# GpSimd instead of VectorE adds the 1e-5 to the layer norm's variances, in an order mapped anew

## The chip, the cores and the metric

One core of a Trainium2 chip. The time is the device time of the whole launch in microseconds (us): the lower the better. A core has a matrix engine (TensorE, PE in the profile), three engines for elementwise work, VectorE (DVE), ScalarE (ACT) and GpSimd (POOL), a SyncE (SP) that here only issues DMAs, and 16 DMA engines. Every engine runs its own list of instructions in order; between engines there are semaphores.

## The reference

S = 2048 rows, D = 640 columns, F = 1536 hidden rows; everything that comes in or goes out is bf16.

```
x = A_q
g = sigmoid((x * gate_w).sum(-1))                 # one gate per row

k_shift[s] = sum over t of A_k[s-3+t] * shift_k[:, 3-t]     # 4 taps along the rows
kv = k_shift * A_v
y  = causal convolution of kv with ssm_k along S  # by rfft of length 4096, column by column
a  = x * (y + kv * ssm_D)

h = (x - mean(x)) / sqrt(var(x) + 1e-5)           # layer norm, along D
u = gelu(w1^T h + b1)                             # w1: 2048 x 1536, mixes the rows
b = w2^T u + b2                                   # w2: 1536 x 2048

out = g * a + (1 - g) * b
```

The 1e-5 of the change is the one in h.

## The kernel before

**How work is written and ordered.** The builder does not issue instructions where it describes them. Each operation goes into a plan with its engine, its operands and an estimate of its cost, through a few helpers: `ts` (tensor with one or two scalars; the profile gives its line, L660 with one scalar and L661 with two), `tt` (two tensors, L653), `act` (ScalarE, L691), `copy` (L668), `memset` (L671), DMAs (L265 on SP's queue, L262 for adding DMAs on GpSimd's queue, L722 and L728 for gathers and scatters of rows), and `pe` (a group of matmuls, L311). There are 853 operations. At the end `plan.run(ORDER)` (L1405; `run` is at L399) emits them in the order of a list written out by hand, `ORDER` (L433 to L470), which is a permutation of the 853 numbers. Since each engine runs its own instructions in the order in which they are emitted, `ORDER` sets the sequence on every engine and in both DMA queues, and also which of four PSUM slots a group of matmuls gets: `run` hands a group the free slot that was used longest ago. A tracker compares the operands of each operation with earlier ones and puts in the semaphore waits. The cost that an operation carries in the plan is not used when it is emitted.

**The layer norm (L901 to L933).** The 2048 rows are 16 tiles of 128 rows, in nine groups: two of one tile, then seven of two. For each group:

- SP loads x (L265).
- VectorE takes two statistics per tile, of 320 columns each (L919), and one aggregate per tile (L921), which leaves mean and variance in `mv`.
- `vpe` = variance + 1e-5, one `ts` for the group (L923, seen as L660), on VectorE.
- `rstd` = vpe to the power -0.5, on GpSimd (L924).
- h = (x - mean) * rstd: for 12 tiles by VectorE (L661), for 4 tiles (6, 10, 14 and 15) by ScalarE, for which VectorE first makes `nmr` = -mean * rstd (L661, 128x1).

**The other stages.** They run interleaved.

- *Filter.* `ssm_k` comes in four blocks of 512 (`wnat`). `w_turn` adds and subtracts mirrored halves on VectorE (`en`) and turns the result into `eo`, for the first two blocks by matmuls whose results ScalarE and VectorE evict in turn (L1006 is VectorE's eviction), for the others by a transposing DMA. `w_freq` multiplies `eo` with cosine and sine tables (`TFc`, `TFs`, with small ones like `TS`), and ScalarE evicts to `W`. The tables are made at the start from index tables (`idx`, `frow`, `hcol` on VectorE and GpSimd, sines on ScalarE); `AFc`, `AFs` are tables for kv alike.
- *kv.* `k` is loaded turned (`kT`), shifted and weighted by matmuls with diagonals (`dg`), evicted by ScalarE (`ks`), turned back by DMA (`kt`); VectorE multiplies it with `v` and forms `es`. `a_freq` (af0 to af3, one per block) multiplies with `AFc`/`AFs`, ScalarE evicts to `A`, VectorE adds A's sum.
- *Products.* `pair(j, m)` multiplies block j of kv's frequencies with block m - j of the filter's and accumulates in `Z` (VectorE, `tt` and `Z` by turns). `inverse(m)` multiplies Z with the inverse tables, and ScalarE evicts to `pq`.
- *MLP.* `mlp1` forms h^T w1 in four sets of three 128-row slices, accumulating over the 16 tiles of h, and ScalarE applies gelu (`gT`). `mlp2(q)` multiplies with `w2` in eight slices of 256 columns; two buffers take turns, so a slice's load (768 KB on SP's queue) can start only after the last matmul of the slice before the last. ScalarE evicts with scale 1 - g and bias.
- *Epilogue.* VectorE forms y from `pq`, multiplies with `xe` (x times the gate, by ScalarE), and the result is added to `out` by adding DMAs or, for odd groups of rows, by way of a scratch `rows_o`. For the last block VectorE adds everything itself (`fin`, L1327) and writes with two plain writes and two scatters.

**GpSimd's list around the layer norm** has, besides the nine powers, the index casts and masks of the start, the memset of 16 columns behind each `wnat` block, and small copies such as that of `TS`.

Of the kernel before, what the change touches and what calls it, by code (L numbers as in the profile page):

```python
# [12 lines left out]
ALU = mybir.AluOpType  # L13
# [409 lines left out]
def _checked(items, offs, base, top):  # L423
# [7 lines left out]


ORDER = [  # L433
# [36 lines left out]
]  # L470


def _build(nc, A_q, A_k, A_v, A_shift_k, A_ssm_k, A_ssm_D, B_x, B_w1, B_b1, B_w2, B_b2, gate_w, out):
# [18 lines left out]
    with ExitStack() as es:  # L492
# [152 lines left out]
        def nel(ap):  # L645
            k = 1
            for st, ct in list(ap.ap)[1:]:
                k *= ct
            return k
# [5 lines left out]
        def ts(out_, in0, s1, s2, op0, op1, pr, eng="DVE", cost=None):  # L655
            c = cost if cost is not None else (0.07 + nel(out_) / 1920.0 if eng == "DVE" else 0.4 + nel(out_) / 900.0)

            def f(e):
                if s2 is None:
                    return e.tensor_scalar(out_, in0, s1, None, op0=op0)  # L660
                return e.tensor_scalar(out_, in0, s1, s2, op0=op0, op1=op1)  # L661

            rr = [in0] + [a for a in (s1, s2) if isinstance(a, bass.AP)]
            return vop(eng, c, f, rr, [out_], pr, kind="ts")
# [105 lines left out]
        b = bufs  # L770
# [135 lines left out]
        for gi, (t0, cnt) in enumerate(groups):  # L906
            pr = 1.0 + t0 * 0.08
            plan.tag = f"ln{t0}"
            dma(x[:, t0:t0 + cnt, :], rows(A_q, t0, cnt, D, 0, D), f"x{gi}", pr)
            for t in range(t0, t0 + cnt):  # L910
                if LMODE[t] == "A":
                    act(h[:, t, :], x[:, t, :], ACT.Copy, pr, scale=-1.0 / (D * sq), acc=b["mv"][:, t, 0:1])
                    act(h[:, t, :], x[:, t, :], ACT.Square, pr, scale=1.0 / sq, bias=b["mv"][:, t, 0:1],
                        acc=b["mv"][:, t, 1:2])
                    continue
                for c in range(2):
                    o_ = b["stats"][:, t, c * 6:(c + 1) * 6]
                    i_ = x[:, t, c * HD:(c + 1) * HD]
                    vop("DVE", 0.393, (lambda o_, i_: lambda e: e.bn_stats(o_, i_))(o_, i_), [i_], [o_], pr, kind="bn")  # L919
                o_, i_ = b["mv"][:, t, :], b["stats"][:, t, :]  # L920
                vop("DVE", 0.11, (lambda o_, i_: lambda e: e.bn_aggr(o_, i_))(o_, i_), [i_], [o_], pr, kind="ba")  # L921
            sl = slice(t0, t0 + cnt)
            ts(b["vpe"][:, sl], b["mv"][:, sl, 1], 1e-5, None, ALU.add, None, pr, cost=0.07)  # L923
            vop("POOL", 0.7, (lambda o_, i_, e_: lambda e: e.tensor_tensor(o_, i_, e_, ALU.pow))(  # L924
                b["rstd"][:, sl], b["vpe"][:, sl], bc(c_mh, [[8, 128], [0, cnt]])), [b["vpe"][:, sl], c_mh], [b["rstd"][:, sl]], pr, kind="pow")
            for t in range(t0, t0 + cnt):
                if LMODE[t] == "D":
                    ts(h[:, t, :], x[:, t, :], b["mv"][:, t, 0:1], b["rstd"][:, t:t + 1],
                       ALU.subtract, ALU.mult, pr + 0.1, cost=0.36)
                else:  # L930
                    o_, a_, r_ = b["nmr"][:, t:t + 1], b["mv"][:, t, 0:1], b["rstd"][:, t:t + 1]
                    ts(o_, a_, r_, sq if LMODE[t] == "A" else -1.0, ALU.mult, ALU.mult, pr, cost=0.07)
                    act(h[:, t, :], x[:, t, :], ACT.Identity, pr, bias=o_, scale=r_)  # L933
# [504 lines left out]
```

## Time and profile before

| | us |
|---|---|
| three runs | 190.6, 190.5, 192.65 (median 190.6) |
| the profiled execution, whole time | 190.98 |
| its span (first to last instruction) | 189.2 |
| TensorE busy | 178.8 (95%) |
| VectorE busy | 175.5 (93%) |
| ScalarE busy | 125.5 (66%) |
| GpSimd busy | 35.2 (19%) |

How the rows that follow are read. `L660` is line 660 of the kernel. A row of a group reads: line, engine, operation, output <- inputs (partitions x elements, type), how often (x7), then after the bar the busy time of all in us, the mean of one in ns, and the idle time of the engine just before them with what ended it. A row of the timeline reads: start in us from the start of the span, duration in us, engine, line, operation, operands, count, and in brackets the idle time before it and its releaser. A row of the chain (start, duration, engine, operand) belongs to the chain of work that ended last, followed back from the last instruction. Rows with a stretch (`22.80:42.00`) give the length, the busy time of each engine with its instructions, the granted clock of TensorE, the share of the DMA engines and the GB/s. Rows of DMA issues give the queue, the KB each and the median time from issue to landing. Idle time of an engine that is not the bottleneck costs nothing.

### The profile page before, as it was taken

How to read it: one execution, taken by the hardware profiler on the slowest of the kernel's cores; microseconds unless marked ns; L12 is line 12 of the kernel's file. 1: busy time of each engine (PE TensorE's matmuls, PEld its weight loads, DVE VectorE, ACT ScalarE, POOL GpSimd, SP SyncE). 2: the span in 40 equal slices, each digit the busy share in tenths (PEclk: the TensorE clock that was granted, in tenths of full speed). 3: DMA queues.
4: the chain of work that ended last, by engine and by line, in shares of the span. 5: the costliest groups of instructions: out<-in, count | busy, mean ns of one | idle time of the engine just before them, and what ended most of it. 6: DMA issues, size and time to landing. Idle time of an engine off the chain costs nothing.

```text
span 189.2 us, 3940 instructions
## 1 busy us (share of the span) xinstructions
PE 178.8 (95%) x1590; PEld 123.0 (65%) x1590; DVE 175.5 (93%) x246; ACT 125.5 (66%) x202; POOL 35.2 (19%) x68
## 2 busy tenths in 40 slices
PE   7778899999999999999999999999999899999992
PEld 2345666566667757777767777777667577777771
DVE  7999999999999999999899999999999999997352
ACT  4978999787699489439823047706778482495930
POOL 8366076610000000101000000000005003110732
PEclk9999999999999999999999999999999999999999
DMA  5999999798996876787948998997988976979992
GB/s 155 315 325 272 130 152 282 221 222 190 236 326 129 196 202 181 151 248 164 232 67 221 231 243 197 219 242 205 309 280 224 225 226 221 232 215 240 175 166 69
DMA packets 81094, 40.37 MB, mean 213 GB/s; under 512 B 40051, under 2 KB 80884, under 8 KB 81076
## 3 DMA queue, kind: packets, MB, share of 16 engines
q1 hardware_dynamic: 78340, 37.18, 78.5%
q0 software_dynamic: 2736, 2.95, 9.3%
q8 instruction: 12, 0.20, 0.4%
q14 instruction: 6, 0.05, 0.1%
HBM read 26.03 MB, written 7.54 MB: 177 GB/s over the span
## 4 chain that ended last, share of the span: by engine, by line
PE 61%; DVE 22%; ACT 4%; issue 4%; DMA 4%; POOL 2%; POOLq 1%; DVEq 0%
PE pp L311 61%; DVE stats L919 6%; DMA w<-in_B_w_dram 4%; DVE v L653 3%; DVE en L653 3%; DVE es L653 2%; DVE idx L660 2%; DVE W L653 2%; ACT pq L691 1%; POOL rstd L924 1%; ACT xe L691 1%; DVE h L661 1%; DVE eo L1006 1%; DVE mv L921 1%; DVE A L653 1%
## 5 line engine op out<-in xcount | busy, mean ns | idle before, releaser
L311 PE MATMUL pp<-h,w 128*128 128x320 bf16 x384 | 57.1, 299 | 0.2
L311 PE MATMUL pp<-gT,w 128*128 128x320 bf16 x336 | 48.4, 299 | 0.9 <-DMA w<-in_B_w_dram 0.9
L311 PEld LDWEIGHTS pp<-h,w 128*128 128x128 bf16 x384 | 36.8, 98 | 15.9 <-issue 1.8
L311 PEld LDWEIGHTS pp<-gT,w 128*128 128x128 bf16 x336 | 32.6, 98 | 14.0 <-DMA w<-in_B_w_dram 1.4
L653 DVE TENSOR_TENSOR tt<-A,W 128x3840 bf16<-128x3840 bf16 (+2 forms) x16 | 27.8, 1738 | 0.3
L691 ACT ACTIVATE A<-pp 128x640 bf16<-128x640 f32 x32 | 21.3, 700 | 9.3 <-PE pp L311 9.3
L653 DVE TENSOR_TENSOR Z<-Z,tt 128x3840 bf16<-128x3840 bf16 (+1 forms) x14 | 26.2, 1868 | 0.2
L262 POOL DMA_DIRECT2D out_dram<-xe x3 | 3.8, 1252 | 73.0 <-DVE Z L653 68.4
L691 ACT ACTIVATE o<-pp,c,omg 128x640 bf16<-128x640 f32 x13 | 11.2, 881 | 6.8 <-PE pp L311 6.4
L691 ACT ACTIVATE ks<-pp 128x512 bf16<-128x512 f32 (+1 forms) x24 | 11.1, 518 | 6.1 <-PE pp L311 6.1
L691 ACT ACTIVATE gT<-pp,bf 128x640 bf16<-128x640 f32 x12 | 9.4, 792 | 8.2 <-PE pp L311 8.1
L691 ACT ACTIVATE xe<-xe,gg 128x640 bf16<-128x640 bf16 x16 | 12.7, 827 | 2.4 <-DMA xe<-rows_q 1.2
L919 DVE BATCH_NORM_STATS2 stats<-x 128x6 f32<-128x320 bf16 x32 | 13.7, 472 | 0.0
L653 DVE TENSOR_TENSOR Z<-A,W 128x3840 bf16<-128x3840 bf16 x6 | 12.8, 2154 | 0.9 <-PE pp L311 0.8
L691 ACT ACTIVATE pq<-pp 128x640 bf16<-128x640 f32 x16 | 10.3, 702 | 4.8 <-PE pp L311 4.8
L671 POOL MEMSET W<- 1x640 bf16 x4 | 2.7, 665 | 50.9 <-ACT nq L691 49.6
L691 ACT ACTIVATE W<-pp 128x640 bf16<-128x640 f32 x18 | 12.0, 722 | 0.1
L653 DVE TENSOR_TENSOR W<-W 128x2560 bf16<-128x2560 bf16 x8 | 11.9, 1486 | 0.0
L653 DVE TENSOR_TENSOR y<-pq 128x1280 bf16<-128x1280 bf16 (+1 forms) x10 | 6.6, 688 | 4.5 <-ACT pq L691 4.5
L311 PE MATMUL pp<-kT,dg 64*64 64x256 bf16 x320 | 10.5, 271 | 0.3 <-ACT Wo L691 0.3
L311 PE MATMUL pp<-eo,TFc 128*128 128x320 bf16 x48 | 8.9, 300 | 1.1 <-ACT TFc L691 1.1
L653 DVE TENSOR_TENSOR Z<-Z 128x1280 bf16<-128x1280 bf16 (+1 forms) x16 | 9.9, 653 | 0.1
(147 smaller groups left out, 303.6 us busy)
## 6 DMA issues: line engine op xcount, KB each, us to landing
w<-in_B_w_dram SPq DMA_DIRECT2D x24, 256.0 KB, 4.1
w<-in_B_w_dram SPq DMA_DIRECT2D x8, 768.0 KB, 5.1
wnat<-in_A_ssm_k_dram SPq DMA_DIRECT2D x4, 640.0 KB, 5.7
x<-in_A_q_dram SPq DMA_DIRECT2D x7, 320.0 KB, 6.3
out_dram<-o SPq DMA_DIRECT2D x6, 320.0 KB, 6.1
v<-in_A_v_dram SPq DMA_DIRECT2D x4, 320.0 KB, 4.5
rows_q<-in_A_q_dram SPq DMA_DIRECT2D x8, 160.0 KB, 3.2
xe<-in_A_q_dram SPq DMA_DIRECT2D x4, 320.0 KB, 5.8
```

The lines of the kernel that those rows point to most:

```text
L262: ins = engobj.dma_start(out_ap, in_ap, accum_op=ALU.add)
L311: ins = self.nc.tensor.matmul(ps_ap, lhsT=lhsT, rhs=rhs, start=start, stop=stop)
L653: return vop(eng, c, lambda e: e.tensor_tensor(out_, in0, in1, op), [in0, in1], [out_], pr, kind="tt")
L660: return e.tensor_scalar(out_, in0, s1, None, op0=op0)
L661: return e.tensor_scalar(out_, in0, s1, s2, op0=op0, op1=op1)
L671: return vop(eng, 0.03 + nel(ap) / 1200.0, lambda e: e.memset(ap, val), [], [ap], pr, kind="ms")
L691: return e.activation(out_, src, func, **kw)
L919: vop("DVE", 0.393, (lambda o_, i_: lambda e: e.bn_stats(o_, i_))(o_, i_), [i_], [o_], pr, kind="bn")
L921: vop("DVE", 0.11, (lambda o_, i_: lambda e: e.bn_aggr(o_, i_))(o_, i_), [i_], [o_], pr, kind="ba")
L924: vop("POOL", 0.7, (lambda o_, i_, e_: lambda e: e.tensor_tensor(o_, i_, e_, ALU.pow))(b["rstd"][:, sl], b["vpe"][:, sl], bc(c_mh, [[8, 12 ...
L1006: vop("DVE", 0.74, lambda e: e.tensor_copy(dst, src()), [src], [dst], 0.3, ps=[p_], kind="ev")
```

## The change

Two places. The addition of 1e-5 goes to GpSimd, where it stands ahead of the power that reads its result; the cost beside it is the plan's estimate. And `ORDER` is replaced by another permutation of the same 853 operations; of its 38 lines two are shown.

```diff
 ORDER = [
-    0, 3, 7, 10, 62, 1, 2, 5, 9, 8, 242, 13, 11, 241, 14, 31, 12, 206, 19, 137, 26, 4, 15, 21,
...
-    852, 844, 797, 792, 798, 793, 794, 848, 849, 838, 840, 839, 841,
+    0, 8, 5, 3, 7, 137, 2, 11, 1, 241, 4, 10, 6, 12, 153, 13, 14, 31, 32, 206, 21, 33, 285, 19,
...
+    832, 791, 843, 792, 836, 793, 844, 837, 794, 838, 840, 839, 841,
 ]
...
             sl = slice(t0, t0 + cnt)
-            ts(b["vpe"][:, sl], b["mv"][:, sl, 1], 1e-5, None, ALU.add, None, pr, cost=0.07)
+            ts(b["vpe"][:, sl], b["mv"][:, sl, 1], 1e-5, None, ALU.add, None, pr, eng="POOL", cost=0.25)
             vop("POOL", 0.7, (lambda o_, i_, e_: lambda e: e.tensor_tensor(o_, i_, e_, ALU.pow))(
                 b["rstd"][:, sl], b["vpe"][:, sl], bc(c_mh, [[8, 128], [0, cnt]])), [b["vpe"][:, sl], c_mh], [b["rstd"][:, sl]], pr, kind="pow")
```

The new list changes the sequence on every engine, far beyond the layer norm. What it does at the places that the prediction speaks of:

- *The start.* Ahead of VectorE's second eviction of `eo` the same 24 statistics stand in both orders, and 12 aggregates instead of 5; two additions fewer stand there, and the write to `AFs` stands ahead of it. Three statistics stand ahead of the third table's index.
- *The last groups of the layer norm.* GpSimd does two additions, three powers and the copy of `TS` in one run; VectorE has eight h and two `nmr` between its last aggregate and the h that reads the last power.
- *w2.* The numbers of matmuls between the last use of a w2 buffer and its next use are 48 to 66 (66 for the fifth slice, 56 before).
- *The third block.* One accumulation into Z and one y of the epilogue stand on VectorE between the last matmuls of af2 and the sum of its A.
- *The end.* 24 matmuls of `mlp2` stand behind the inverse of the last scatter's rows, instead of 12.

68 rows, old and new, of the table ORDER are left out of this document.

## The prediction, made before the changed kernel was run

> **What bounds the kernel now.** I read the page first, then the chain that ended last, then the busy time by stretches.
>
> ```profile
> span 189.2 us, 3940 instructions
> PE 178.8 (95%) x1590; PEld 123.0 (65%) x1590; DVE 175.5 (93%) x246; ACT 125.5 (66%) x202; POOL 35.2 (19%) x68
> ```
> ```profile
> 49.74 92.22 PE pp L311 x858
> 141.96 6.96 DMA w<-in_B_w_dram
> ...
> 148.96 23.55 PE pp L311 x172
> ```
> ```profile
> 8.20:22.80 14.60, 11.75 (x163) 8.14 (x163) 14.60 (x45) 12.67 (x22) 6.58 (x8) 1.00 1.14 260
> 22.80:42.00 19.20, 18.87 (x196) 12.14 (x192) 19.10 (x52) 17.42 (x32) 10.13 (x12) 1.00 0.95 211
> 42.00:58.00 16.00, 15.64 (x112) 10.40 (x110) 15.85 (x25) 13.19 (x21) 0.12 (x1) 1.00 0.90 244
> 58.00:148.00 90.00, 90.00 (x846) 64.32 (x843) 88.73 (x67) 54.19 (x94) 3.62 (x4) 1.00 0.87 210
> ...
> 149.00:185.50 36.50, 36.50 (x268) 26.04 (x268) 28.93 (x42) 21.68 (x29) 8.12 (x8) 1.00 0.86 201
> ```
>
> In the stretches the columns are TensorE, weight loads, VectorE, ScalarE, GpSimd, then the granted clock (1.00 throughout). Three things are to be seen. Up to 22.8 VectorE is busy in all 14.60 us and TensorE waits for it. From 22.8 to 185.5 TensorE is hardly ever idle: 0.33 us up to 42, 0.36 up to 58, nothing up to 148 or from 149 on; the chain shows what lies between, a load of w that the matmuls at 148.96 waited for. And VectorE stays close behind it (88.73 of 90 us). The matmuls of both kernels are the same, so the time is: when TensorE's dense run begins, its holes, and what lies behind its last matmul. The page's execution took 190.98 us, 1.78 more than its span, which I leave alone; it lies 0.4 above the median of the runs, 190.6.
>
> **The nine additions.** What leaves VectorE and what comes to GpSimd:
>
> ```profile
> L660 DVE TENSOR_SCALAR vpe<-mv 128x2 f32<-128x2 f32 x7 | 1.1, 155 | 0.0
> ```
> ```profile
> 23.19 0.26 DVE L921 BATCH_NORM_AGGREGATE mv<-stats 128x2 f32<-128x12 f32 x2
> 23.41 0.17 DVE L660 TENSOR_SCALAR vpe<-mv 128x2 f32<-128x2 f32 x1
> 23.49 0.20 DVE L921 BATCH_NORM_AGGREGATE mv<-stats 128x2 f32<-128x12 f32 x1
> ```
> ```profile
> L671 POOL MEMSET wnat<- 128x16 bf16 x4 | 0.5, 117 | 3.6 <-DVE mv L921 2.8 <-DVE en L653 0.8
> L668 POOL CAST hcol<-hcol_i 128x2 f32<-128x2 int32 x1 | 0.4, 357 | 0.0
> L660 POOL TENSOR_SCALAR idp<-id_i 128x128 bf16<-128x128 int32 x1 | 0.9, 854 | 0.0
> L924 POOL TENSOR_TENSOR rstd<-vpe,cst 128x2 f32<-128x2 f32 x7 | 5.3, 809 | 7.0 <-DVE vpe L660 6.9
> ```
>
> Seven additions take two tiles of rows, two more take one (the powers show the nine groups, below). On VectorE one is 0.155 us long, but the next instruction starts 0.08 us after it (23.41 to 23.49): instructions overlap there. Nine of them free 9 x 0.08 = 0.7 us, at most 9 x 0.155 = 1.4, at least nothing. The trace shows no such addition on GpSimd. Its nearest row is the cast of two columns, 0.357; the ends are the memset, 0.117, and the mask over 128 columns, 0.854. I take 0.36: same width, same count.
>
> Whether GpSimd then holds up h is decided at the last groups. In the changed order, counted from T, the end of VectorE's last aggregate, VectorE still runs eight of its h and two nmr before the h that needs the last power:
>
> ```profile
> 28.84 0.80 DVE L661 TENSOR_SCALAR h<-x,mv,rstd 128x640 bf16<-128x640 bf16 x2
> 29.55 0.20 DVE L661 TENSOR_SCALAR nmr<-mv,rstd 128x1 f32<-128x1 f32 x1
> ```
> ```profile
> L668 POOL COPY TS<-TFs 128x128 bf16<-128x128 bf16 x1 | 0.3, 287 | 0.1
> ```
>
> Two h take from 28.84 to 29.55, 0.355 each to the next start, and an nmr is 0.20 long, somewhat less to the next start: eight h and two nmr take 2.8 + 0.3 = 3.1 us. GpSimd begins its last run about 0.8 us before T (two h and an nmr lie between the last two aggregates) with two additions, three powers and the copy of TS: 2 x 0.36 + 3 x 0.81 + 0.29 = 3.4, done at T + 2.6. That is 0.5 us early, so I cost GpSimd's part at nothing. The cover is those eight h; with additions of 0.85 and powers of 1.08 (the longest, below) the run takes 5.2 and VectorE is 1.3 us late.
>
> Do the engines lengthen each other?
>
> ```profile
> 24.84 2.08 POOL L924 TENSOR_TENSOR rstd<-vpe,cst 128x2 f32<-128x2 f32 x3 [6.87 <-DVE vpe L660]
> 27.69 2.49 POOL L924 TENSOR_TENSOR rstd<-vpe,cst 128x2 f32<-128x2 f32 x3
> ```
> ```profile
> L661 DVE TENSOR_SCALAR h<-x,mv,rstd x12: 392/438/445, 26.5 to 32.7; 128x640 bf16<-128x640 bf16 x12
> L924 POOL TENSOR_TENSOR rstd<-vpe,cst x9: 561/698/1077, 10.8 to 29.2; 128x2 f32<-128x2 f32 x7, 128x1 f32<-128x1 f32 x2
> ```
>
> Three powers took 2.08 us beside VectorE's statistics and 2.49 beside its h; the longest single one was 1.077. The h beside them were not lengthened (392 to 445 ns). [...]
>
> **The new order: the start.** TensorE's dense run begins behind the second eviction of eo by VectorE:
>
> ```profile
> 21.60 0.81 DVE L1006 CAST eo<-pp 128x640 bf16<-128x640 f32 x1
> ```
> ```profile
> 5.54 0.49 DVE L660 TENSOR_SCALAR idx<-frow,hcol 128x512 int32<-128x512 int32 x1 [0.32 <-ACT adx L691]
> ```
>
> Ahead of this eviction the changed kernel has the same 24 statistics, but twelve aggregates instead of five, one write to AFs more and two additions fewer. An aggregate costs 0.11 (23.19 to 23.41 for two, with the next start): 7 x 0.11 + 0.07 - 2 x 0.08 = +0.7. Against it, three statistics now stand ahead of the third table's index, which covers the 0.32 us wait for ScalarE and some 0.2 of small waits behind it. Net +0.2. Seven of the nine additions stood behind this point: they are hidden by a TensorE that is busy 18.87 of the next 19.20 us. **+0.2**, bounds -0.5 and +0.7.
>
> **The wait for w2.**
>
> ```profile
> 148.96 1.26 PE L311 MATMUL pp<-gT,w 128*128 128x320 bf16 x8 [0.89 <-DMA w<-in_B_w_dram]
> 154.95 9.94 PE L311 MATMUL pp<-gT,w 128*128 128x320 bf16 x72
> ```
> ```profile
> 140.70 1.22 SPq L265 DMA_DIRECT2D rows_o<-xe  x2
> ```
> ```profile
> w<-in_B_w_dram SPq DMA_DIRECT2D x8, 768.0 KB, 5.1
> ```
>
> 72 matmuls take 9.78 us to the next start, 0.136 each. The fifth slice's load stood behind two writes of rows_o in SP's queue and took 6.96 us (chain); between the last use of its buffer and its first use stand 56 matmuls, 7.6 us. In the changed order these gaps are 48 to 66 matmuls: for this slice 66, 9.0 us, and for the shortest, the fourth, 48 and some small ones, 7.4 us, in which SP is held about 1 us by another load and a transfer, which leaves 6.4 for a median landing of 5.1. **-0.9**, bounds -0.9 and +0.5.
>
> **A new tight round trip.** The last matmuls of af2 feed VectorE's sum A, and all of its work up to the last Z feeds the last stage's inverse.
>
> ```profile
> 121.11 0.43 PE L311 MATMUL pp<-v,AFs 128*128 128x320 bf16 x2
> 122.32 1.49 DVE L653 TENSOR_TENSOR A<-A 128x2560 bf16<-128x2560 bf16 x1
> 123.73 2.15 DVE L653 TENSOR_TENSOR Z<-Z,tt 128x3840 bf16<-128x3840 bf16 x1
> ```
> ```profile
> 167.72 2.09 DVE L653 TENSOR_TENSOR Z<-Z 128x640 bf16<-128x640 bf16 x5
> ```
>
> Now VectorE needs 122.32 to 169.81, 47.5 us, and TensorE wants the last Z at 171.8, 50.2 us after 121.54. In the changed order one 2.15 us Z and one y of 0.74 stand ahead of A, so VectorE needs 44.6, with the eviction 45.4. TensorE has 324 matmuls of 128x320 between, 44.0, and 1.0 of gate work: 45.0. VectorE is late by 0.4. **+0.4**, bounds 0 and +2 (should a load of v hold VectorE on the way).
>
> **The end.**
>
> ```profile
> 185.27 1.01 DVE L1327 SCALAR_TENSOR_TENSOR xe<-pp,omg,xe 128x320 bf16<-128x320 f32 x2
> 185.64 1.01 POOL L728 DMA_INDIRECT out_dram<-xe,rev  x1 [3.53 <-DVE xe L653]
> 185.85 0.83 SPq L265 DMA_DIRECT2D out_dram<-xe  x2
> ```
> ```profile
> out_dram<-xe SPq DMA_DIRECT2D x2, 80.0 KB, 1.9
> out_dram<-xe,rev POOLq DMA_INDIRECT x2, 2.9
> ```
>
> The scatter lands at 185.64 + 2.9 = 188.5, the last plain write at about 188.3. In the changed order 24 matmuls (3.3 us) stand behind those of the last scatter instead of 12, so only the plain write is left: **-0.2**, bounds -0.3 and 0.
>
> **Sum.** +0.2 - 0.9 + 0.4 - 0.2 = -0.5: 190.98 becomes 190.5. The runs' median lay 0.4 lower than that execution; I forecast the middle, **190.3 us**: no change that 2% (3.8 us, about what a measurement of this kernel can tell from no change) would show.
>
> **Rivals.**
> *GpSimd becomes the bound of h (0.2), slower.* It decides from additions over 0.6 us: then the run passes the eight h. For it speaks 2.49 against 2.08, against it the 0.5 us of cover. VectorE is 1.3 late at the last h and 0.3 more where the memset of wnat stands behind two additions that wait for an aggregate (two of 0.85 and 0.1 against 1.5 us of VectorE work). All of it passed on: 190.3 + 1.6 = 191.9.
> *A transfer or buffer is late in the dense part (0.2).* TensorE has nothing to gain between 58 and 148, where its idle time is 0, and the new order sets every load anew. The wait for w2 stays (+0.9) and the round trip is late by its upper bound (+1.6): 192.8; two such places: 195.
> *Everything fits (0.12), faster.* Neither the round trip nor the 0.33 and 0.36 us of idle time return, and the start gains 0.5 instead of losing 0.2: 190.3 - 0.4 - 0.7 - 0.7 = 188.5.
>
> **How the numbers follow.** The forecast has 0.48, with 189.4 to 191.4 as its own range. From 188.6 to 193.6 the range takes in all of the first rival, most of the second and the edge of the third; some 0.15 is left out, most of it above. Slower by over 2% (above 194.4) is the second rival with two places: 0.1. Faster by over 2% (below 186.8) lies beyond the third: 0.04. Within: 0.86.
>
> **What would show it.** GpSimd's rows at the helper's line with vpe, near 0.36 us each; no vpe on VectorE; the second eviction of eo near 21.8 and TensorE's run on eo near 23.0; no wait of TensorE for w2; a wait of up to half a microsecond for Z at the inverse near 170; scatters that end ahead of the plain write. Wrong would make it: h waiting for rstd, VectorE idle between 26 and 32, or TensorE idle over 1 us anywhere from 58 on.

## The result and the profile after

The changed kernel took **191.72 us** (median of 22 executions, 190.78 to 194.49), the kernel before 190.41 (22 executions beside it, 190.11 to 192.65). The ratio is 1.0045, 95% interval 1.0024 to 1.0067: slower by 0.45%, where 0.2% faster was forecast. The time lies inside the stated range; the sign is wrong. (The ratio leaves out executions more than 1.5% above the fastest; the median of 22 has them in.)

Two things make up the 191.72. Eleven of the 22 executions ran with a mean granted clock of 0.985 or more; their median is 190.92, half a microsecond above before. The other eleven had 0.971 to 0.982 and took 191.36 to 194.49. Of the 117 executions of before that lie beside the experiments below, none had a clock under 0.991.

The profiled execution of the changed kernel took 190.81 us. Its page, first lines:

```profile
span 189.0 us, 3937 instructions
PE 180.1 (95%) x1590; PEld 124.2 (66%) x1590; DVE 175.4 (93%) x237; ACT 126.2 (67%) x202; POOL 36.8 (19%) x77
```

The busy time by stretches (TensorE, weight loads, VectorE, ScalarE, GpSimd, granted clock):

```profile
8.20:22.80 14.60, 11.66 (x141) 8.02 (x142) 14.60 (x50) 12.11 (x21) 8.42 (x17) 0.88 1.15 246
22.80:42.00 19.20, 18.16 (x199) 11.75 (x200) 19.02 (x38) 17.19 (x32) 9.49 (x17) 1.00 0.86 206
42.00:58.00 16.00, 16.00 (x117) 11.02 (x116) 14.81 (x20) 13.18 (x21) 0.00 (x0) 1.00 0.92 228
...
149.00:185.50 36.50, 36.50 (x270) 26.02 (x268) 29.49 (x41) 24.09 (x33) 8.24 (x8) 1.00 0.82 202
```

TensorE idles 1.04 us between 22.8 and 42 (0.33 before), and from 42 on there is no hole but 0.24 us. So the loss lies in the start, where the granted clock is 0.88 on the mean. The chain that ended last shows what the start hangs on:

```profile
9.04 1.46 POOL v L722
10.49 0.04 issue
10.53 1.61 POOL vpe L660
12.14 0.07 issue
12.21 0.72 POOL rstd L924
12.94 0.06 POOL TFs L671
12.99 0.46 POOL TFc L671
13.45 0.18 POOL TFs L671
13.63 0.05 issue
13.68 1.08 PE pp L311 x9
14.76 0.02 issue
14.78 0.70 ACT eo L691
15.48 0.81 ACT h L691
16.29 3.06 ACT Wo L691 x5
```

The first addition on GpSimd (`vpe`) took 1.61 us in this chain. Behind it on GpSimd stand a power and three memsets that finish the tables TFs and TFc; TensorE waited for the last of them until 13.68, and ScalarE had to evict later. Beside that addition VectorE ran this (timeline):

```profile
10.56 1.48 DVE L995 TENSOR_TENSOR dg<-id,shd 128x1280 bf16<-128x1280 bf16 x1
```

The other additions cost little: over the nine, the fastest, the median and the longest are 213, 227 and 1597 ns.

```profile
L660 POOL TENSOR_SCALAR vpe<-mv x9: 213/227/1597, 10.5 to 27.4; 128x2 f32<-128x2 f32 x7, 128x1 f32<-128x1 f32 x2
```

**The execution of before was not a typical one.** The forecast counted from 190.98 us, with 0.89 us of TensorE waiting for w2. A second profile of the same kernel, taken among the experiments, took 189.95 us (span 188.1). The last matmuls of before, of its second profile and of the changed kernel, in this order:

```profile
183.75 1.79 PE L311 MATMUL pp<-gT,w 128*128 128x320 bf16 x12
```
```profile
182.67 1.79 PE L311 MATMUL pp<-gT,w 128*128 128x320 bf16 x12
```
```profile
182.73 3.42 PE L311 MATMUL pp<-gT,w 128*128 128x320 bf16 x24
```

TensorE ends at 185.54, 184.46 and 186.15. Against the second profile the change costs 1.7 us up to the last matmul and gives 0.8 back behind it (188.1 - 184.46 = 3.6; 189.0 - 186.15 = 2.8): +0.9 in the span.

### The profile page after: what moved, and what is told of

It is laid out like the page before. It is cut to its first block, busy times and chain, and to the rows that moved or that the text cites. A ratio compares the mean times of both kernels' runs of the same rounds, so it can differ in the third digit from the quotient of the medians.

```text
span 189.0 us, 3937 instructions
## 1 busy us (share of the span) xinstructions
PE 180.1 (95%) x1590; PEld 124.2 (66%) x1590; DVE 175.4 (93%) x237; ACT 126.2 (67%) x202; POOL 36.8 (19%) x77
## 4 chain that ended last, share of the span: by engine, by line
PE 74%; DVE 12%; ACT 8%; POOL 3%; issue 2%; POOLq 0%; DVEq 0%
PE pp L311 74%; DVE Z L653 3%; DVE tt L653 2%; ACT Wo L691 2%; DVE v L653 2%; ACT h L691 1%; ACT eo L691 1%; POOL vpe L660 1%; DVE es L653 1%; DVE idx L660 1%; DVE A L653 1%; ACT ks L691 1%; POOL v L722 1%; DVE xe L653 1%; ACT TFs L691 1%
## 5 line engine op out<-in xcount | busy, mean ns | idle before, releaser
L262 POOL DMA_DIRECT2D out_dram<-rows_o x6 | 7.8, 1361 | 55.3 <-DMA rows_o<-xe 55.3
L311 PE MATMUL pp<-eo,TFs 128*128 128x320 bf16 x48 | 9.6, 329 | 2.8 <-ACT eo L691 2.0
L311 PEld LDWEIGHTS pp<-kT,dg 64*64 64x64 bf16 x320 | 8.1, 105 | 2.8 <-issue 1.6
```

The costliest lines, as they stand in the source:

```text
L262: ins = engobj.dma_start(out_ap, in_ap, accum_op=ALU.add)
L311: ins = self.nc.tensor.matmul(ps_ap, lhsT=lhsT, rhs=rhs, start=start, stop=stop)
```

## The experiments

Times in us; each ratio is to the executions of before on the same chip. "Low clock" counts executions with a mean granted clock below 0.985.

| kernel | n | median | fastest | low clock | ratio to before |
|---|---|---|---|---|---|
| the changed kernel | 22 | 191.72 | 190.78 | 11 | 1.0045 (1.0024 to 1.0067) |
| the same, again | 7 | 191.64 | 190.81 | 0 | 1.0057 (1.0030 to 1.0085) |
| new order, additions on VectorE | 12 | 190.52 | 190.18 | 2 | 0.9989 (0.9962 to 1.0017) |
| old order, additions on GpSimd | 12 | 192.11 | 191.69 | 0 | 1.0071 (1.0041 to 1.0102) |
| old start, new rest | 12 | 192.95 | 190.67 | 1 | 1.0067 (1.0030 to 1.0103) |
| new start, old rest | 12 | 192.29 | 191.13 | 4 | 1.0078 (1.0046 to 1.0109) |
| first addition alone on VectorE | 12 | 190.78 | 190.10 | 1 | 0.9992 (0.9966 to 1.0018) |
| table memsets ahead of it | 12 | 190.30 | 190.10 | 1 | 0.9978 (0.9947 to 1.0009) |
| the same, again | 12 | 190.37 | 189.87 | 3 | 1.0014 (0.9984 to 1.0043) |
| dg later | 12 | 190.68 | 190.30 | 1 | 0.9992 (0.9965 to 1.0020) |
| tables ahead and dg later | 12 | 190.69 | 190.35 | 3 | 1.0001 (0.9969 to 1.0032) |
| ten more matmuls | 12 | 191.51 | 190.73 | 0 | 1.0019 (0.9992 to 1.0045) |
| tables ahead, ten more matmuls | 12 | 190.37 | 189.94 | 0 | 0.9986 (0.9962 to 1.0010) |
| before with six matmuls fewer | 10 | 191.61 | 190.30 | 2 | 1.0031 (1.0001 to 1.0061) |

### Engine or order

The changed kernel's order with the additions on VectorE:

```diff
-            ts(b["vpe"][:, sl], b["mv"][:, sl, 1], 1e-5, None, ALU.add, None, pr, eng="POOL", cost=0.25)
+            ts(b["vpe"][:, sl], b["mv"][:, sl, 1], 1e-5, None, ALU.add, None, pr, cost=0.07)
```

> The changed kernel with its order kept and the nine additions back on VectorE. Two theories for the loss. THE ENGINE: the additions on GpSimd are what costs; in the trace of the changed kernel one of them took 1.60 us (10.53 to 12.13) beside VectorE's product dg, and the table memsets behind it on GpSimd made TensorE wait 0.43 us. Then this kernel loses that and runs at 190.4 us or below, against about 190.9 for the changed one at an undisturbed clock. THE ORDER: what costs is the new sequence of the first 31 us, whatever engine adds; then this kernel stays at 190.7 to 191.2, and the half granted clock between 10 and 14 us is there in some executions too.

190.52 us, ratio 0.9989: the loss is gone. None of the 12 executions is above 193 (7 of the 22 with the additions on GpSimd, but none of the 7 when that kernel was timed again, so their absence alone tells little). The new order alone is worth nothing either way that these runs can tell. The engine costs.

The old order with the additions on GpSimd (the same line, the other way round):

> The kernel before, its order kept, with the nine additions on GpSimd. THE ENGINE: slower than before by 0.5 to 1.5 us (190.8 to 191.8), with single additions of over 1 us beside VectorE's sums of two inputs. THE ORDER: the same as before within 0.3 us (190.0 to 190.6), since seven of the nine additions stand behind the point from which TensorE is dense.

1.0071: slower, by more than the upper end of the expectation in the median (192.11), and not by the way that was expected. No addition was longer than 0.45 us; VectorE waited for the powers instead (its waits, over the execution):

```profile
DVE nmr L661 <- POOL rstd L924: 0.9, 1, 0.9
...
DVE h L661 <- POOL TS L671: 0.7, 1, 0.7
DVE h L661 <- POOL rstd L924: 0.6, 1, 0.6
```

2.2 us of waits that the kernel before has none of (in the row with TS, too, the last power ends at 31.56, just before the h goes on). It is the first rival of the forecast, in the order of before: there GpSimd's additions and powers set the pace of h. That these waits make the loss is argued from this one profile. In neither profile of the changed kernel does an h wait for a power: its order has room for the longer chain.

Next, which part of the order. The orders were cut in two and crossed (the lists, written as formulas):

```diff
+ORDER = OLD[:242] + [i for i in NEW if i not in OLD[:242]]    # old start, new rest; additions on VectorE
```

> The first 242 operations in the order of before (up to the first matmuls on h, at 30.8 us there), all others in the new order, additions on VectorE. THE ORDER, with its loss in the start: the new start reaches the first matmuls on h 2.5 us later (33.9 against 30.8, less 0.6 for 16 matmuls that it has done by then), and the rest of the new order is the better one, so this kernel is the fastest of all, 188.4 to 189.5. If the new rest is no better than the old one: 190.1 to 190.9.

```diff
+ORDER = NEW[:229] + [i for i in OLD if i not in NEW[:229]]    # new start, old rest; additions on GpSimd
```

> The first 229 operations in the new order, all others in that of before, additions on GpSimd. THE ORDER, with its loss in the start: the slowest of all, 191.8 to 192.9, and a low clock in some executions. If start and rest weigh alike: 190.6 to 191.2.

The second came out as expected (192.29), the first did not: 192.95 instead of 188.4 to 190.9. Its profile, of its slowest execution (195.15 us), has waits of TensorE that are new or longer than in the profiles of its parents (the kernel before: 0.2 for es; the new order with the additions on VectorE: 0.6 for a load of w at the same place, the start of the MLP):

```profile
PE pp L311 <- DVE es L653: 1.7, 1, 1.7
PE pp L311 <- DMA kT<-in_A_k_dram: 1.4, 1, 1.4
PE pp L311 <- DMA w<-in_B_w_dram: 1.3, 1, 1.3
```

So crossing orders does not tell what a half is worth: the loads at the start of one half belong to the other. Nothing is concluded from these two.

### The one long addition

Only the first addition that GpSimd does goes back:

```diff
-            ts(b["vpe"][:, sl], ..., pr, eng="POOL", cost=0.25)
+            ts(b["vpe"][:, sl], ..., pr, eng="DVE" if t0 == 14 else "POOL", cost=0.25)
```

> The changed kernel; of the nine additions only the first that GpSimd does (group of tiles 14 and 15, at 10.53 us) goes back to VectorE, eight stay on GpSimd. THE ONE LONG ADDITION: the whole loss hangs on its 1.60 us, since the memsets of the tables stand behind it on GpSimd (the one that TensorE waits for ends at 13.6 us, and at 11.9 with all nine on VectorE); then this kernel is at 190.3 to 190.6 as with all nine on VectorE, and executions above 193 are gone. ALL NINE: the loss is the sum of many; then it stays above 190.75.

No execution is above 193 and the fastest is at 190.10, but the median, 190.78, is above what was expected; its ten slower executions spread from 190.63 to 191.55. That does not settle it. The next does: the memsets (operations 41, 39 and 43) go ahead of the addition (144), nothing else moves.

```diff
-    ..., 144, 56, 48, 259, 145, 208, 53, 267, 41, 39, 58, 105, 251, 43, 268, ...
+    ..., 41, 39, 43, 144, 56, 48, 259, 145, 208, 53, 267, 58, 105, 251, 268, ...
```

> The changed kernel, all additions on GpSimd; the three memsets of the tables TFs and TFc stand ahead of the first addition on GpSimd instead of behind its power. THE ONE LONG ADDITION, by way of what is queued behind it: 190.2 to 190.6, TensorE's wait for TFs (0.43 us) gone. If the addition costs by way of its power and h, or of VectorE being held: no gain, 190.75 to 191.

190.30 us, and 190.37 when it was run again; 0.9978 and 1.0014 against before, with all nine additions on GpSimd. GpSimd's timeline in it:

```profile
10.51 0.09 POOL L671 MEMSET TFs<- 1x1 bf16 x1
10.53 0.52 POOL L671 MEMSET TFc<- 1x512 bf16 x1
11.00 0.20 POOL L671 MEMSET TFs<- 1x128 bf16 x1
11.17 1.02 POOL L660 TENSOR_SCALAR vpe<-mv 128x2 f32<-128x2 f32 x1
12.28 0.72 POOL L924 TENSOR_TENSOR rstd<-vpe,cst 128x2 f32<-128x2 f32 x1
```

The addition is still long, and the memsets, beside the same product on VectorE, are not. TensorE's wait for TFs is gone from this profile, as expected. So the addition costs by what is queued behind it.

> The same kernel as new_tables_first, a second time, beside the changed kernel as it is. If its gain is real: 0.3 to 0.8 us below the changed kernel again, and at or below before (ratio 0.995 to 1.000). If it was chance: within 0.2 us of the changed kernel.

> The changed kernel as it is, timed beside the mended ones. Fastest executions at 190.8 as before, a third or more above 191.5 with a granted clock below 0.985.

The mended kernel stayed 1.27 us below the changed one on the same chip (190.37 against 191.64), which is above the expected 0.3 to 0.8; the expected low clocks of the changed kernel did not come (all seven at 0.991), its loss did.

Then the cause of the length: VectorE's product is moved behind other work of VectorE, 2.4 us of it by the trace (10.69 to 13.08; the expectations say 1.4).

```diff
-    ..., 145, 208, 53, 267, 41, ..., 148, 128, 250, 213, ...
+    ..., 145, 53, 267, 41, ..., 148, 128, 250, 208, 213, ...
```

> The changed kernel with VectorE's product dg (1.48 us, two inputs in memory) moved 1.4 us of VectorE's work later, so that the first addition runs beside statistics. If VectorE's product holds GpSimd up: this addition falls from 1.60 to 0.2 to 0.3 us, and the time to 190.3 to 190.6. If the addition is long for a reason of its own (the first of its kind on GpSimd): it stays above 1 us, and the time at 190.75 to 191.

```profile
10.54 0.26 POOL L660 TENSOR_SCALAR vpe<-mv 128x2 f32<-128x2 f32 x1
```
```profile
13.08 1.48 DVE L995 TENSOR_TENSOR dg<-id,shd 128x1280 bf16<-128x1280 bf16 x1
14.47 0.83 DVE L653 TENSOR_TENSOR en<-wnat 128x1280 bf16<-128x1280 bf16 x1
```
```profile
14.02 2.98 POOL L924 TENSOR_TENSOR rstd<-vpe,cst 128x1 f32<-128x1 f32 x2
```

1.60 became 0.26: the addition is long because of the product beside it. And the stall has moved: the two powers that now fall beside the product and the sums behind it took 2.98 us (1.51 in the changed kernel). The time, 190.68, is a little above what was expected. Both mends together:

> Both mends: the table memsets ahead of the first addition, and VectorE's product dg moved 1.4 us of work later. If the addition matters by what is queued behind it on GpSimd alone, moving dg as well brings nothing: 190.0 to 190.4, like the tables alone. If the length of the addition itself matters too (its power, ScalarE's h of tile 14): 189.6 to 190.0.

190.69 is above both expectations. It is 0.3 above the tables alone in the median, but its ratio to before, 1.0001, is not above theirs, 1.0014: no difference that these runs can tell. Taking the length off the addition brings nothing once the memsets are ahead of it.

The end of the addition goes with that of the product: in the changed kernel the addition ended at 12.13 and the product at 12.04; with the memsets first, 12.19 and 12.11. Each time it ended 0.08 to 0.09 us behind the product, whenever it had started; in the changed kernel it had even started 0.03 us ahead of the product (10.53 and 10.56). The memsets, which have no input, ran beside the product at their usual length: 0.52 and 0.20 with the memsets first, 0.52 and 0.23 in the changed kernel, where the product had ended. By what the product holds the addition up is not shown.

### The clock

```diff
-    NWARM = 15
+    NWARM = 20
...
         pe([p_], [(p_, 0, 512, wz, wzb, True, True)] * NWARM, -400, cost=0.427 * NWARM + 0.9)
+        p_ = _PS()
+        pe([p_], [(p_, 0, 512, wz, wzb, True, True)] * 5, -400)    # ahead of the first matmuls on eo
```

> The changed kernel with ten more matmuls on the constant wz whose results nobody reads: five at the end of the fifteen at the start, five between the second group of turning matmuls (8.5 us) and the first ones on eo (10.4 us), where TensorE idles. THE CLOCK: the half granted clock between 10 and 14 us comes from TensorE's idle time between 7.4 and 10.4 us; then it is gone in nearly all executions (clock 0.995 or more), and with it the executions above 191.3; the fastest stay at 190.8, since there the clock is full already. If the clock falls for another reason, it falls here as often, in about half of the executions below 0.985.

No execution is below 0.985 and none above 191.85, and the fastest is at 190.73, as expected; five of the twelve still have 0.989 to 0.991, where nearly all were expected at 0.995 or more. The median is 191.51, and the clock is not what keeps it high (seven executions at 1.00 took 190.73 to 191.61). Its profile names another cause: VectorE waited for the third block of the filter.

```profile
40.53 1.58 DVE L653 TENSOR_TENSOR en<-wnat 128x1280 bf16<-128x1280 bf16 x2 [1.36 <-DMA wnat<-in_A_ssm_k_dram]
```

That block's buffer lies where `mv` and `nmr` lay, so its load goes out when the last h is done. In the changed kernel (ScalarE's last h, then SP's issue):

```profile
33.35 0.93 ACT L691 ACTIVATE h<-x,nmr,rstd 128x640 bf16<-128x640 bf16 x1
```
```profile
34.38 0.37 SPq L265 DMA_DIRECT2D wnat<-in_A_ssm_k_dram  x1
```
```profile
38.90 1.58 DVE L653 TENSOR_TENSOR en<-wnat 128x1280 bf16<-128x1280 bf16 x2
```

4.5 us from issue to use. In the kernel before the issue stands at 33.21 and the use at 39.65, 6.4 us; in the new order with the additions on VectorE the issue stands at 33.41. A late start thus leaves this load less room. In the kernel with the ten matmuls it was issued at 34.50 and could be used at 40.53, 6.0 us later, and VectorE waited. This is shown in one profile. The changed kernel's second profile comes from its executions at 191.4 to 192.3 (191.64) and has no such wait, so the load doesn't explain them all; there the time was lost at the start, as the clock shows below.

What the clock follows was tried from both sides. First before, with TensorE idle earlier:

```diff
-    NWARM = 15
+    NWARM = 9
```

> The kernel before, its order and its additions kept, with nine matmuls on the constant wz at the start instead of fifteen (their results are not read), so that TensorE idles from about 4.9 to 8.2 us instead of from 6.9. THE CLOCK FOLLOWS TENSORE'S IDLE TIME: the granted clock of most executions falls from 0.996 to 1.000 to below 0.992, by a stretch of about 3.3 us at half clock, and the time rises by 0.3 to 2 us. If the clock falls for another reason than idle time: clock and time as before (190.2 to 190.8).

Five of ten executions had 0.973 to 0.991, and the median rose by 1.1 us. Its profiled execution (190.8 us of span, clock 0.973):

```profile
5.00:8.00 3.00, 0.00 (x0) 0.00 (x0) 2.68 (x8) 2.94 (x5) 1.66 (x8) 0.88 1.04 316
8.00:11.00 3.00, 2.77 (x23) 2.39 (x24) 3.00 (x16) 2.49 (x5) 0.29 (x2) 0.50 1.09 360
11.00:14.00 3.00, 2.10 (x9) 0.95 (x8) 3.00 (x8) 2.09 (x4) 2.80 (x4) 0.50 1.15 312
14.00:17.00 3.00, 3.00 (x13) 1.68 (x12) 3.00 (x11) 1.57 (x3) 2.55 (x3) 0.50 1.13 251
17.00:20.00 3.00, 3.00 (x23) 1.92 (x22) 1.30 (x3) 2.16 (x5) 0.95 (x1) 0.91 1.14 233
```

That is half of them, where most were expected. TensorE was busy for 0.00 us from 5 to 8, and at 8 the clock was down. The clock fell as forecast, but the lost time is not the clock's: the other five executions show 1.00 and took 191.4 to 192.2 us (median 192.00), more than the five with the lower clock (191.10). One candidate was not tried, the start itself. The fifteen matmuls on wz took 4.99 us in one profile (the second with the memsets ahead) and 6.37 in another (the second of before), while the granted clock shows no fall there in either: the second of before has 1.000 over the whole execution, and what the other lacks (0.991) lies between 11 and 15 us (0.57, 0.50, 0.50 and 0.72). So in these two profiles the granted clock doesn't tell how fast the start ran. Then the mended new order with the ten matmuls more:

> The changed kernel with the table memsets ahead of the first addition and with ten more matmuls on wz at the start (five behind the fifteen, five before the first ones on eo; their results are not read). THE CLOCK FOLLOWS TENSORE'S IDLE TIME: no execution below 0.985 (3 of 12 and 1 of 12 without the ten), and the time of the best ones of the tables alone, 190.1 to 190.4, in nearly all. If not: a clock of 0.97 to 0.985 in some executions as before.

All twelve executions are at 0.999 or 1.000, as expected; their times, 189.94 to 191.12, spread further than the 190.1 to 190.4 that were expected of nearly all. As far as these runs show it, the clock goes with how busy TensorE is at the start: from 8 to 11 us it was busy for 2.38 us in the profile of this kernel (clock 1.00) and for 1.30 and 1.31 in the two of the changed kernel (0.991 both). By what the five executions at 1.00 of the kernel with fewer matmuls lost their time stays open. In the changed kernel's first profile the stretch at half clock is one of 3.42 us: the clock was 0.72, 0.50, 0.50 and 0.57 of full in the four microseconds from 10 to 14 (0.56 + 1 + 1 + 0.86, if it was full or half). In the second profile of the changed kernel the fall came later, behind a longer wait for the memset:

```profile
13.67 0.72 PE L311 MATMUL pp<-eo,TFs 128*128 128x320 bf16 x4 [1.72 <-POOL TFs L671]
```
```profile
14.00:15.00 1.00, 0.67 (x8) 0.41 (x6) 1.00 (x3) 0.30 (x1) 0.84 (x3) 0.93 1.28 232
15.00:18.00 3.00, 2.54 (x10) 1.49 (x11) 3.00 (x12) 2.59 (x5) 1.83 (x3) 0.50 1.12 264
18.00:19.00 1.00, 1.00 (x8) 0.64 (x6) 1.00 (x4) 0.67 (x2) 0.00 (x0) 0.86 1.04 338
```

0.14 + 3 + 0.28 = 3.42 us again, now over matmuls that were due: the matmuls that wait for W at 28.36 in the first profile do so at 29.25 in the second, 0.9 us later. Both profiles have 0.991, one stretch each; the profile with 0.973 has 10.26 us at half (0.72 + 9 + 0.54 by the rows from 5 to 20), three times as long. A stretch is not a loss by itself: with the additions on VectorE five of the twelve executions have 0.990 or 0.991, and they took 190.18 to 190.48 us.

In the changed kernel TensorE had not been idle all the time ahead of the falls. These are the 3.41 us, about the length of a fall, before the one at 10.44 (11 - 0.56) and before the one at 14.86 (15 - 0.14); the first number behind the comma is TensorE's busy time:

```profile
7.03:10.44 3.41, 1.12 (x13) 0.60 (x12) 3.41 (x13) 2.22 (x5) 1.52 (x2) 1.00 0.97 303
```
```profile
11.45:14.86 3.41, 1.50 (x16) 0.96 (x14) 3.41 (x12) 2.06 (x4) 3.16 (x9) 1.00 1.27 268
```

TensorE was busy for 1.12 and 1.50 us of the 3.41. What sets off a fall, and why the changed kernel has 0.973 in one execution and 1.000 in another, no run here shows.

### Before once more

> The kernel before, for a second profile. The forecast took off 0.9 us for TensorE's wait for the fifth slice of w2, as the one profiled execution showed it (190.98 us, above the median 190.4). If that wait belongs to every execution: 0.7 to 1.0 us again. If it belongs to that execution: below 0.5 us, and with it a time near 190.3.

No wait for w2 at all, 189.95 us. The profiles of the old order with the additions on GpSimd and with six matmuls fewer have none either (their waits for w, where there is one, stand at the start of the MLP). The 0.89 belonged to that one execution.

None of these kernels beats the kernel before beyond its interval; the best, with the table memsets ahead, are level with it.

## Why the prediction was wrong, step by step

- **"I cost GpSimd's part at nothing" is the step that failed.** It was argued at one place, the last groups of the layer norm, and there it held: no h waited for a power in either profile, and GpSimd's last power ended 2.84 us after VectorE's last aggregate (29.77 against 26.93), where 2.6 was forecast. What the step left out is the other end of GpSimd's list: three table memsets that TensorE needs stand behind the first addition, which took 1.60 us, and TensorE waited for them until 13.68.
- **The price of an addition, 0.36 with ends 0.117 and 0.854,** held for eight (the median of the nine is 0.227) and missed the ninth, whose 1.60 is nearly twice the upper end. The two rows that read memory, the cast and the mask, come from moments without a long two-input operation on VectorE (it made the index table, 2.34 to 4.06 us, from one tensor at a time, and the first statistics). Whether the engines lengthen each other was looked at for powers beside statistics and h (2.08 and 2.49 us for three), and h was found unharmed (392 to 445 ns); the operation to look for was dg, of 1.48 us.
- **The rival with GpSimd as the bound** (0.2, 191.9) had the right engine, but the wrong place: in the changed kernel it decides at the start by way of the tables, not at h, so that 191.9 lies close to the median is luck. At h it decides in the old order.
- **The start, +0.2.** The second eviction of eo came at 21.97, as forecast (21.8). But TensorE was no longer bound by it: its dense run on eo began at 24.40 instead of 23.0, behind ScalarE, which was late from the tables on.
- **The wait for w2, -0.9.** Right that no such wait is in the changed kernel's profiles, wrong that it was there to be won: the second profile of before has none. The term was measured on an execution 0.4 us above the median, and the text saw that difference without asking which of its waits made it.
- **The round trip to the last inverse, +0.4:** no wait near 170. VectorE's work behind af2 was the bound at an earlier place: the chain that ended last runs from the matmuls ahead of 124.45 by way of A and VectorE's list to the matmuls on v at 145.10, where TensorE waited 0.24 us.
- **The end, -0.2:** the direction was right and the size too small. 3.6 us behind the last matmul became 2.8, with the last scatter issued 1.5 us ahead of TensorE's end (184.64) instead of 0.1 behind it (185.64 in the first profile of before), so that the plain write is the last to land (two issued from 186.18 on, 1.6 us to landing in the median; the scatter, at 2.9, by about 187.5).
- **The clock** was taken as 1.00 throughout and no row was thought to change it. The changed kernel's executions below 0.985 took 0.4 to 3.6 us more than the median of its others; how much of that is the clock's is not shown.
- **What a measurement can tell** was put at 2%, 3.8 us. The 22 executions of each kernel told 0.45% from no change.

Summed as measured against the second profile: +1.7 up to the last matmul, -0.8 at the end. With the additions on VectorE the same order is level with before within its interval, and so it is with them on GpSimd and the table memsets ahead; so what is lost is the first addition's.

## What to carry to other kernels

When an operation moves to another engine, look at everything that is queued behind each of its instances on that engine, first of all at the start, and at what the neighbour engine runs at that moment: one addition of nine, by the memsets behind it, cost what was lost here. Before a wait in a profile is counted as a gain, ask whether a typical execution has it; a profile slower than the median by half of the wait was the sign here that it doesn't. Look at the clock behind a gap of TensorE too: in the second profile of the changed kernel one of 1.72 us was followed by 3.42 us at half clock over matmuls that were due, and the matmuls that wait for W came 0.9 us later than in the first, where the fall was over at 13.86.

## What was not expected of the hardware

- An addition over 128 x 2 numbers on GpSimd took 1.60 us beside a product of two inputs on VectorE (the changed kernel) and 0.26 when the product came later; the median of the nine is 0.227. Two powers took 2.98 us beside that product and the sums behind it, instead of 1.51. Memsets beside the same product kept their length (0.52 and 0.20, against 0.52 and 0.23).
- The granted clock fell to one half for 3.42 us in both profiles of the changed kernel, and for 10.26 us in that of before with six matmuls fewer; in the changed kernel TensorE was busy for 1.12 and 1.50 us of the 3.41 before, the second 44%. In the changed kernel 17 of the first 22 executions and all seven later ones have a clock of 0.991 or less; of the 117 of before four have 0.991 and none less. Between 7 and 10 us TensorE was busy for 1.14 and 0.73 us in the two profiles of the changed kernel, for 1.64 and 2.08 in those of before.
- Six matmuls on a constant, left out at the very start, cost the kernel before 1.1 us in the median (ratio 1.0031, interval 1.0001 to 1.0061).
